# The long convolution as one transform of length 2048 with two DMA-shuffled stages, beside dilated sliding attention, on one core

## The chip, the cores and the metric

One core of one Trainium2 chip. The metric is device microseconds of one execution; the lower, the better.

## What is computed

Two independent parts, joined along the last axis. S = 2048 positions, D = 576 channels, bf16.

```python
# part A: 32 heads of 18 channels, 8 keys per query at distances 0, 2, .., 14
q, k, v = split(x @ wqkv)
logits = einsum("bhsd,bhswd->bhsw", q, k[s - 2*w]) * 18 ** -0.5   # masked where s - 2w < 0
a = einsum("bhsw,bhswd->bhsd", softmax(logits), v[s - 2*w]) @ wo
# part B: a 4-tap filter, a gate, a causal convolution over all 2048 positions, a gate
kv = (sum over t of k_pad[t:t+S] * shift_k[:, 3-t]) * v
y = irfft(rfft(pad(kv, 2*S)) * rfft(pad(ssm_k, 2*S)))[:S] + kv * ssm_D
b = q * y
out = concatenate([a, b], axis=-1)
```

## The kernel before

All work is cut into named jobs, and the string `ORDER` lists them in the order in which they are issued; each engine runs its own part of that list in program order. PSUM is used as four slots of two banks (`banks`); a job that needs a slot waits until the job that held it has been copied out.

Part A: `q`, `k`, `v` jobs project (columns of `wqkv` against the transposed x, 512 positions at a time; an `a` and a `b` half, the copy out at the end of `b`). `L` jobs are pair products of q and shifted k on VectorE, `G` jobs sum them over channels on TensorE. `sm..a` to `sm..d` are the softmax. `D` jobs spread the weights by DMA, `V` jobs weigh the shifted v on VectorE, `A` jobs sum over the eight keys on TensorE by an identity matrix, and `O` jobs multiply by `wo`, copy out and store. The first projections and the transposes of the first half of x stand ahead of ORDER.

Part B: `T` jobs (`taps`) form kv on VectorE in four blocks of 512 positions: multiply by the taps, add, gate. `M` folds each block with its mirror image. `x` jobs transform the four blocks, `F` and `K` fold and transform the filter's four blocks (loaded by `Lf` as DMA transposes), `U`, `Tx`, `Tk` and `ak`, `ax` prepare sums of parts, partly by DMAs that add. `p` jobs multiply a block's spectrum by a filter block's, with three products for one complex one; `z` jobs add the products up on TensorE, `i` and `b` transform back, `g` gates with q and stores. `Ex` loads ScalarE's table with Exp and Ln and `S1`, `I` make the transforms' tables from sines. ScalarE copies nearly all results out of PSUM. `Lk`, `Lv`, `Lf`, `Lw`, `Wl`, `Q` are loads, on SP's queue or POOL's.

Of the kernel before, what the change touches and what calls it, by code (L numbers as in the profile page):

```python
# [12 lines left out]
ALU = mybir.AluOpType  # L13
# [7 lines left out]
    T0 k03a' T1 S1 k03b I1 k02a k02b Lk2 Lv2 I0 k00a' Lk3 Lv3 M01 X5 k00b q10a Ex q10b Lf3 T2 Lo3 q13a' q13b  # L21
    k10a k10b T3 k13a' Lf2 k13b q12a q12b N2 Lo2 k01a M10 k01b Lf1 M00 k11a k11b q11a M11 q11b Lf0 N3 Lw SV L001
    k12a M20 k12b x001 M21 x021 q24a x020 q24b x000 Lo1 k24a Fr Lo0 Z2 N1 RG3 k24b RG2 F3 RG0 F2 L000 K310 G000
    K311 K210 K211 L002 K313 G001 RG4 F1 G002 L003 G003 K302 L004 G004 K301 L010 K212 L011 K303 K213 K203 N0 F0
    L012 K200 K300 G010 L013 K201 K312 K202 RG1 G011 G012 K113 K103 G013 L014 G014 K112 K102 K101 L100 K100 K010
    K111 K110 sm0a K001 K013 sm0b v24a' L101 v24b L102 G100 L103 G101 K012 sm0c sm0d U3 U2 K000 K011 K003 G102
    K002 D0 D1 v11a v11b G103 L104 G104 ak00 M30 v12a' v12b ak02 v01a ak01 L110 G110 M31 L111 G111 v01b v00a'
    L112 G112 L113 Wl v00b G113 x031 U1 L114 G114 V04 v10a' v10b A04 sm1a sm1b v02a v02b v03a' sm1c v03b x201
    V10 V11 sm1d V12 A10 v13a' v13b D2 x330 x310 x301 V13 A11 V20 V21 x200 x331 x230 x010 x221 A20 x321 V22 x210
    x011 V23 D3 V34 ax02 x220 x030 x300 D4 A21 V40 V41 A34 D5 O000' x211 V42 x320 x231 x111 x131 Tx2 A40 V43  # L30
    x120 x101 ax00 x130 ax01 V50 x121 x311 O001 A41 V51 O100' p000 x100 x110 O010 A50 V52 z000 O011' V53 O101
    A51 Tk2 p010 z010 ax10 O020' O021 p020 z020 O110' ak10 i000 p200 i02880 Q0 p100 z100 p101 p110 p111 Q1 z101
    i02881 i001 p121 p120 O111 z110 p201 z111 z120 p210 z121 O120 p211 z200 z210 z211 p212 z212 z201 p202 z202
    Tx3 p220 Tk3 p221 O030' p222 O121 b0288 z220 p301 z221 O031' p302 b00 z222 p303 i200 i100 g0 Q2 p300 y300
    p312 i12880 i201 i101 i12881 z300 z301 z303 p310 p311 y310 O130 b10 b1288 p313 g1 Q3 p322 O131' z310 p320
    z311 p321 z313 i22880 i300 b20 y320 p323 i22881 i301 b2288 g2 z320 z321 z323 b30 i3384L g30 g3384
"""

LHOMES = (0, 1, 2, 0, 1, 2, 0, 1, 2, 0, 1, 2, 0, 1, 0, 1, 0, 1, 0, 1)
VHOMES = (0, 1, 2, 0, 1, 2, 0, 1, 2, 0, 1, 2, 0, 1, 2, 0, 1, 2)  # L40
OHOMES = (0, 1, 1, 0, 2, 0, 1, 0)
JOINED = ("300 310 320").split()
PHOMES = (0, 1, 2, 3, 0, 1, 2, 3, 0, 4, 1, 2, 3, 0, 4, 1, 2, 3, 0, 1, 2, 3, 0, 1, 2, 3, 0, 1, 2, 3)


def view(t, offset, dims):

    return bass.AP(tensor=t.tensor, offset=t.offset + offset, ap=[list(t.ap[0])] + [list(d) for d in dims])


@with_exitstack
def kernel(
# [24 lines left out]

# [3 lines left out]

    NBL, BL = 4, 512  # L90


    GORD = [0, 2, 1, 3]
    HD = 288
    HB = 4 * D
    QTR = 768
    TH = 192
# [12 lines left out]
    jobs = {}  # L110

    xw = main.tile([128, 12 * HB], BF16, name="xw")
    XO = 8 * BL
    TB = main.tile([128, XO + 4 * BL], BF16, name="TB")
    TK = view(TB, 0, [[2 * BL, 2], [BL, 2], [1, BL]])
    TX = view(TB, XO, [[BL, 4], [1, BL]])
    TI = main.tile([128, 4, 2, 256], BF16, name="TI")
    XG = (9, 0, 3, 6)
    KVS = (0, 2, 1, 8)

    def kv_of(i):
        return view(xw, HB * KVS[i], [[D, 4], [1, D]])
# [26 lines left out]
    tB = sp1.tile([128, 8 * D], BF16, name="tB")  # L149
    skrow = tB[0:97, 0:4 * D]  # L150
# [17 lines left out]
    Ks = main.tile([128, 12 * HB], BF16, name="Ks")  # L168
    xnat = view(Ks, 4 * HB, [[HB, 4], [D, 4], [1, D]])
    n_all = view(Ks, 8 * HB, [[1, 4 * HB]]).bitcast(I32).rearrange("p (n f) -> p n f", n=9)  # L170

    def k_at(m, part):
        return 3 * HB * (3 - m) + HB * part

    def kTok(m):
        return view(Ks, k_at(m, 2), [[D, 4], [1, D]])
    kjs, vts = [], []

    def load_x(qtr):
        nc.sync.dma_start(xnat[:, qtr], xf[512 * qtr:512 * qtr + 512, :].rearrange("(sb p) c -> p sb c", p=128))  # L180
# [3 lines left out]
    def load_k(i):  # L184

        eng = nc.sync
        kj = sp1.tile([128, 7, D], BF16, name="kj", bufs=2)
        r0 = BL * i
        low = [(0, 64)]
        if i == 0:  # L190
            nc.gpsimd.memset(kj[0:1, 0:3, :], 0.0)
            nc.gpsimd.dma_start(kj[0:1, 3:7, :], kf[0:4, :].unsqueeze(0))
            low = [(1, 49), (49, 64)]
        for a, b in ((3, 7), (0, 3)) if i == 0 else ((0, 7),):
            for p0, p1 in low:
                eng.dma_start(kj[2 * p0:2 * p1:2, a:b], bass.AP(
                    tensor=kf.tensor, offset=kf.offset + (r0 + 4 * p0 - 3 + a) * D,
                    ap=[[4 * D, p1 - p0], [D, b - a], [1, D]]))
            eng.dma_start(kj[1:128:2, a:b], bass.AP(tensor=kf.tensor, offset=kf.offset + (r0 + 256 + 3 - a) * D,
                                                    ap=[[4 * D, 64], [-D, b - a], [1, D]]))  # L200
        kjs.append(kj)

    def load_v(i):
        vt = sp1.tile([128, 4, D], BF16, name="vt", bufs=2)
        nc.sync.dma_start(vt[0:128:2], vf[BL * i:BL * i + 256, :].rearrange("(p c) d -> p c d", c=4))
# [9 lines left out]
    fr_i = n_all[:, 8, :].rearrange("p (a b) -> p a b", a=4)
    rp_i = main.tile([128, 8], I32, name="rp_i")
    rp = main.tile([128, 8], FP32, name="rp")
    nc.gpsimd.iota(rp_i[:, 0:4], pattern=[[128, 4]], base=0, channel_multiplier=1)
    nc.gpsimd.iota(rp_i[:, 4:8], pattern=[[4, 4]], base=1, channel_multiplier=8)
    for gi, g in enumerate(GORD):  # L220
        sg = 1 - 2 * (g & 1)
        nc.gpsimd.iota(fr_i[:, gi, :], pattern=[[8 * sg, 128]], base=4096 * (g & 1) + sg * (2 * g + 1),
                       channel_multiplier=0)
    ones128 = sp1.tile([128, 128], BF16, name="ones128")
    nc.gpsimd.memset(ones128[:], 1.0)
    ident = main.tile([128, 128], BF16, name="ident")
    nc.gpsimd.affine_select(ident[:], ones128[:], pattern=[[1, 128]], compare_op=ALU.is_equal, fill=0.0,
                            base=0, channel_multiplier=-1)

    load_w(nc.sync, 0)  # L230
    load_x(1)

    def turn_x(h):

        r0 = 1024 + 512 * h
        nc.sync.dma_start(xnat[:, 2 + h, :, 512:576], xf[r0:r0 + 512, 512:576].rearrange("(sb p) c -> p sb c", p=128))
        nc.sync.dma_start_transpose(view(xw, 6 * HB + 512 * h, [[1024, 4], [1, 512]]), xf[r0:r0 + 512, 0:512])

    load_k(0)
# [896 lines left out]
```

## Time and profile before

| what | value |
|---|---|
| time, median of 3 runs | 206.23 us (206.15 to 206.59) |
| span of the profiled execution | 204.6 us |
| TensorE (PE) busy | 196.9 us, 96% |
| VectorE (DVE) busy | 192.3 us, 94% |
| ScalarE (ACT) busy | 155.6 us, 76% |
| GpSimd (POOL) busy | 60.8 us, 30% |
| DMA | 38.48 MB, mean 188 GB/s |

The span runs from the first to the last instruction of the profiled execution, and that execution's own time is known by this span only; the runs' times include what lies around it. "Busy" counts an engine's instructions of work. The chain that ended last is followed back from the last instruction, step by step, to what released each step. A group of instructions is shown as line, engine, operation, out<-in, shape and count, then busy time in us, mean ns of one, and the idle time before them.

### The profile page before, as it was taken

What the parts mean: (1) busy time and instruction counts of PE and PEld (TensorE: products, weight loads), DVE (VectorE), ACT (ScalarE), POOL (GpSimd) and SP (SyncE); (2) the same over time, 40 slices, a digit from 0 to 9 for tenths busy, and PEclk for the clock granted to TensorE, in tenths of its full rate; (3) what the DMA queues carried; (4) which work ended last, traced back from release to release, by engine and by line L of the source; (5) the groups of instructions that cost most, each with busy time, mean ns of one, the idle gap of its engine ahead of it and who ended that gap; (6) DMA issues with size and microseconds to landing.
All of it is one profiled execution on the core that took longest, in us unless ns stands there. A gap on an engine that the chain in (4) does not pass through costs nothing.

```text
span 204.6 us, 5004 instructions
## 1 busy us (share of the span) xinstructions
PE 196.9 (96%) x2074; PEld 109.9 (54%) x2074; DVE 192.3 (94%) x146; ACT 155.6 (76%) x223; POOL 60.8 (30%) x106
## 2 busy tenths in 40 slices
PE   7999999999989999999999999999999999999990
PEld 2543544334455646543245556776666767766660
DVE  7559999999999999999999999999999999899992
ACT  4788995678899999966578678886778767767760
POOL 8989500011348581400380000004090001030300
PEclk9999999999999999999999999999999999999997
DMA  6999899989509869999899990879989303944555
GB/s 197 280 293 306 175 289 373 214 177 281 169 3 146 111 82 185 167 180 222 157 235 216 248 244 34 141 183 334 186 227 233 100 28 122 227 130 145 153 182 150
DMA packets 34916, 38.48 MB, mean 188 GB/s; under 512 B 17523, under 2 KB 28911, under 8 KB 34894
## 3 DMA queue, kind: packets, MB, share of 16 engines
q1 hardware_dynamic: 26668, 24.29, 46.5%
q0 software_dynamic: 5760, 11.36, 29.5%
q10 hardware_dynamic: 2466, 2.51, 3.6%
q8 instruction: 16, 0.26, 0.5%
q14 instruction: 6, 0.05, 0.1%
HBM read 13.11 MB, written 4.72 MB: 87 GB/s over the span
## 4 chain that ended last, share of the span: by engine, by line
PE 88%; DMA 3%; ACT 2%; DVE 2%; issue 1%; SPq 1%; DVEq 0%
PE ps_proj L322 18%; PE ps_fx L682 8%; PE ps_wo L888 8%; PE ps_z L975 8%; PE ps_inv L1010 7%; PE ps_acc L824 7%; PE ps_fk L567 5%; PE ps_log L720 5%; DMA Ks<-in_A_x_dram 3%; PE ps_proj L333 3%; PE ps_proj L326 3%; PE ps_proj L439 3%; PE ps_fk L568 3%; PE ps_fold L545 2%; PE ps_wo L880 1%
## 5 line engine op out<-in xcount | busy, mean ns | idle before, releaser
L322 PE MATMUL ps_proj<-xw 128*128 128x512 bf16 x160 | 38.5, 380 | 0.0
L706 DVE TENSOR_TENSOR av<-qk 128x4096 bf16<-128x4096 bf16 (+1 forms) x16 | 31.7, 2014 | 0.1
L322 PEld LDWEIGHTS <-xw 128*128 128x128 bf16 x160 | 13.9, 98 | 19.4 <-issue 5.7
L988 ACT ACTIVATE av<-ps_z 128x768 bf16<-128x768 f32 x23 | 17.2, 811 | 6.5 <-PE ps_z L975 6.0
L517 DVE TENSOR_TENSOR tB<-kj,skb 128x4608 bf16<-128x4608 bf16 (+1 forms) x8 | 19.3, 2416 | 0.1
L950 DVE TENSOR_TENSOR qk<-xw,Ks 128x2304 bf16<-128x2304 bf16 x14 | 18.9, 1354 | 0.3 <-PE ps_z L975 0.3
L684 ACT ACTIVATE xw<-ps_fx 128x576 bf16<-128x576 f32 x32 | 18.6, 665 | 0.3 <-PE ps_fx L682 0.2
L618 ACT ACTIVATE Ks<-ps_fk 128x576 bf16<-128x576 f32 x32 | 18.6, 699 | 0.2 <-PE ps_fk L568 0.2
L355 ACT ACTIVATE qk<-ps_proj 128x1024 bf16<-128x1024 f32 x14 | 14.3, 1023 | 5.2 <-PE ps_proj L333 2.8
L888 PE MATMUL ps_wo<-qk 128*128 128x288 bf16 x128 | 17.9, 287 | 0.0
L626 POOL DMA_DIRECT2D Ks<-Ks x8 | 10.1, 1426 | 26.0 <-PE ps_back L1059 19.3
L682 PE MATMUL ps_fx<-xw,TB 128*128 128x288 bf16 x128 | 17.7, 287 | 0.0
L567 PE MATMUL ps_fk<-Ks,TB 128*128 128x384 bf16 x62 | 16.5, 327 | 0.1
L824 PE MATMUL ps_acc<-av,ident 64*64 64x512 bf16 x160 | 15.3, 378 | 0.0
L1010 PE MATMUL ps_inv<-av,TI 128*128 128x288 bf16 (+1 forms) x112 | 15.2, 292 | 0.0
L568 PE MATMUL ps_fk<-Ks,TB 128*128 128x192 bf16 x62 | 15.2, 246 | 0.0
L682 PEld LDWEIGHTS <-TB 128*128 128x128 bf16 x128 | 11.9, 98 | 5.9 <-issue 2.7
L888 PEld LDWEIGHTS <-qk 128*128 128x128 bf16 x128 | 11.7, 98 | 5.4 <-issue 2.7
L355 ACT ACTIVATE v<-ps_proj 128x1024 bf16<-128x1024 f32 x9 | 9.3, 1033 | 6.5 <-PE ps_proj L322 4.5
L813 DVE TENSOR_TENSOR av<-Ks,v 128x4096 bf16<-128x4096 bf16 x6 | 13.5, 2286 | 0.0
L827 ACT ACTIVATE qk<-ps_acc 128x1024 bf16<-128x1024 f32 x8 | 8.2, 1024 | 6.7 <-PE ps_acc L824 6.7
L1010 PEld LDWEIGHTS <-TI 128*128 128x128 bf16 x112 | 10.6, 98 | 4.2 <-issue 1.1
(195 smaller groups left out, 441.6 us busy)
## 6 DMA issues: line engine op xcount, KB each, us to landing
Ks<-Ks POOLq DMA_DIRECT2D x8, 576.0 KB, 7.8
TB<-av SPq DMA_DIRECT2D x12, 256.0 KB, 5.4
kj<-in_B_k_dram SPq DMA_DIRECT2D x6, 504.0 KB, 7.0
vt<-in_B_v_dram SPq DMA_DIRECT2D x8, 288.0 KB, 5.3
Ks<-av SPq DMA_DIRECT2D x8, 256.0 KB, 5.6
out_dram<-qk ACTq DMA_DIRECT2D x5, 288.0 KB, 3.7
Ks<-in_A_x_dram SPq DMA_DIRECT2D x2, 576.0 KB, 5.4
xw<-in_A_wqkv_dram SPq DMA_DIRECT2D x2, 576.0 KB, 6.2
```

The source lines that it names most:

```text
L322: nc.tensor.matmul(ps[:, jp, :], wq(kb, comp, 128 * ct, 128), xT(kb, 1024 * jj + 512 * jp, 512), **se)
L355: nc.scalar.activation(view(t, o + pad + 1024 * jj, [[512, 2], [1, 512]]), ps[:], ACT.Copy)
L517: tt(to, view(kj, row * D, [[D, n], [D, 4], [1, D]]), view(skb, row * D, [[D, n], [0, 4], [1, D]]), ALU.mult)
L567: nc.tensor.matmul(o[:, 0:2], w, rhs[:, 0:2], start=start, stop=stop)
L568: nc.tensor.matmul(o[:, 2], w, rhs[:, 2], start=start, stop=stop)
L618: nc.scalar.activation(view(Ks, k_at(m, cs ^ (m & 1)) + 96 * gi, [[768, 3], [384, 2], [1, 96]]), acc3(ps), ACT.Copy, scale=(PSG, MSG)[cs][ ...
L682: nc.tensor.matmul(ps[:, pm, 0:HD], TX[:, 2 * pm + c, 128 * gi:128 * gi + 128], kv[:, 2 * c + pm, HD * h:HD * h + HD], start=(c == 0), sto ...
L706: tt(view(P, at, [[step, 4], [256, nj], [1, 256]]), view(t, o + 256 * hh, [[0, 4], [512, nj], [1, 256]]), view(tk, ok + 2 + 8 * ug + 256 * ...
L824: nc.tensor.matmul(acc[64 * o:64 * o + 64, h, :], ident[64 * h:64 * h + 64, 64 * h:64 * h + 64], view(P[s], 256 * u, [[2048, 2], [1, 256]] ...
L888: nc.tensor.matmul(ps[:, r, 0:HD], oT(hh, j + 2 * r, t)[:, o:o + 128], wo[:, t // 2, t % 2, HD * h:HD * h + HD], start=(t == 0 and not fli ...
L950: tt(product_home(n), view(xw, HB * XG[i] + QTR * t, [[HB, 3], [1, QTR]]), view(Ks, k_at(j - i, 0) + QTR * t, [[HB, 3], [1, QTR]]), ALU.mult)
L1010: nc.tensor.matmul(ps[:, c, 0:n], TI[:, sl, pm, 128 * c:128 * c + 128], Yall(j % 2, pm, sl, slice(c0, c0 + n)), start=(pm == 0 and sl == 0 ...
```

## The change

Part B is written anew, and ORDER with it; the jobs of part A keep their content.

- `t` (8) and `s` (12) take the place of `T`: VectorE multiplies by the taps, TensorE adds the four taps by an identity matrix into PSUM, VectorE gates out of PSUM. Half of the rows hold positions in reversed order, so k and v are loaded in blocks of 32 partitions.
- `x` (18) and `f` (18) are a first stage of the transform, 64 rows at a time; after each, DMAs on POOL's queue put 144 KB each into four partitions (32 DMAs for x, 32 for f). `X` and `Y` (18 each) are the second stage, in place, with a small matrix. `F` (8) turns the filter, now loaded straight, by TensorE transposes.
- `p` (18) multiplies four parts on VectorE, `z` (18) is the inverse's first stage with 32 more such DMAs, `y` (9) its last stage, gated by q out of PSUM and stored.
- Tables: two index tables are multiplied out on POOL, and `Sw`, `Sx`, `Sf` take sines of them on ScalarE; `Tw`, `Tt` transpose.
- The v projection reads its weights 9 columns apart, so the regrouping copies (`RG`) go. `Ex` stands in the last line of ORDER.

The order of issue begins, turns and ends so:

```
Sw t01 t00 Lw s00 s01 s02 k03a k00a k00b t10 k02a k02b k03b XT Sx t11 s10 s12 s11 q10a t20 q10b Sf k01a k01b
Tw q11a q11b t21 s22 s20 s21 x0 k12a k12b x1 x2 q12a q12b x3 q13a q13b t30 t31 s30 s31 L002 x4 x5 k10a k10b
...
G111 F2 Dr f0 G112 D0 G113 G114 F1 f1 f2 sm1a f3 F4 sm1b F5 F6 F3 f4 F7 f5 f6 f7 D1 f8 V04 sm1c sm1d f9 f10
X3 f11 f12 V10 V11 A04 V12 D2 X1 f13 f14 f15 f16 f17 X11 A10 V13 D4 X13 X9 V20 A11 Y0 V21 Y2 V22 Y14 p0 Y1
...
O000 p16 p17 z16 z17 O010 V43 A41 z8 V50 Tt Q11 O001 V51 V52 A50 V53 O011 y3 y0 y5 A51 y1 O020 O021 O030
O031 y2 y4 y6 O110 O111 O100 Ex O101 y7 O130 O131 y8 O120 O121
```

New functions, cut to their core:

```python
def tap_sums(c, p):
    ...
    kv = view(R5, 2 * D * c + lo, [[8 * D, 2], [1, 384]])
    tt(kv, ps[:, :, 0:384], kv, ALU.mult)

def first_stage(name, T, src, ring, size, place, to, at):
    ...
    for a, w in cut(at, 512, size):
        copy_out(name, view(WR, ring + a % size, [[size, 2], [1, w]]), ps[:, :, a - at:a - at + w])
    ...
                nc.gpsimd.dma_start(to[pi:128:32, :].rearrange("p (r c) -> p r c", c=D),
                                    view(WR, ring + size * hh + D * g % size, [[1, D]]))

def second_stage(name, w, t, p):
    ...
            nc.tensor.matmul(ps[64 * o:64 * o + 64, h, :], w[r], view(t, HALF * o + 512 * p, [[1, 512]])[r],
                             start=True, stop=True, tile_position=(64 * h, 64 * o))
    copy_out(name, view(t, 512 * p, [[HALF, 2], [1, 512]]), ps[:])

def spectral_product(p):
    tt(view(*product_home(p), [[1024, 2], [512, 2], [1, 512]]), view(VB, 512 * p, [[HALF, 2], [0, 2], [1, 512]]),
       view(FB, 512 * p, [[0, 2], [HALF, 2], [1, 512]]), ALU.mult)

def last_stage(u):
    ...
    qB = view(FB, 1024 * u, [[512, 2], [1, 512]])
    tt(qB, ps[:], qB, ALU.mult)

def indices(at, m):
    nc.gpsimd.tensor_tensor(view(words(at, 2048), 0, [[32, 64], [1, 32]]), view(m, 0, [[1, 64], [0, 32]]),
                            view(vec, 0, [[0, 64], [1, 32]]), ALU.mult)

-    load_v(0)
+    load_v(0, 4)      # 8 DMAs of 32 partitions, in place of 2
     load_k(1)         # 4 DMAs, in place of 2
     turn_x(0)
     turn_x(1)
-    load_v(1)
+    load_k(2)
+    load_k(3)
+    load_v(4, 4)
```

`copy_out` is ScalarE's copy here for every job, as the list of exceptions is empty.

More of the change, by code (lines that the diff above doesn't have):

```diff
@@ L31 @@
[L31 to L35, printed above, removed]
@@ L110, with job @@
     jobs = {}
[L112 to L122, printed above, removed]
+    late = set(VEVAC.split())
+    def job(name, fn, *args):
+        assert name not in jobs
+        jobs[name] = partial(fn, *args)
@@ new lines, in copy_out @@
+    def copy_out(name, to, of):
+        if name in late:
+            nc.vector.tensor_copy(to, of)
+        else:
+            nc.scalar.activation(to, of, ACT.Copy)
+    qk = main.tile([128, 4 * S + 1024 + 4 * KW + KWH], BF16, name="qk")
+    VB = main.tile([128, 2 * HALF], BF16, name="VB")
+    FB = main.tile([128, 2 * HALF], BF16, name="FB")
+    WR = main.tile([128, 2 * HALF + 8 * D], BF16, name="WR")
+    R5 = main.tile([128, HALF], BF16, name="R5")
+    VV = main.tile([128, 4 * KW + KWH], BF16, name="VV")
@@ L215 @@
[L215 to L223, printed above, removed]
@@ new lines, in pieces_of, with load_v, load_filter @@
+    def pieces_of(t, pitch, c0, hh, s, b, i0, n):
+        f = 2 * i0 + (hh if b == 0 else 1 - hh)
+        return rows_of(t, pitch, c0, 63 - 16 * b - f if s else 16 * b + f, n, -2 if s else 2)
+    def load_v(i0, n):
+        for p, hh, s in BLOCKS:
+            for b in range(2):
+                nc.sync.dma_start(view(R5, 8 * D * b + D * i0, [[D, n], [1, D]])[p:p + 32],
+                                  pieces_of(vf, D, 0, hh, s, b, i0, n))
+    def load_filter(kb):
+        at = (R5, 2048 * kb) if kb < 4 else (WR, HALF)
+        p = min(128, 576 - 128 * kb)
+        nc.sync.dma_start(view(*at, [[1, S]])[0:p], B_ssm_k[128 * kb:128 * kb + p, :])
@@ new lines, in turn_walls, with turn_table @@
+    def turn_walls():
+        ps, slot = banks("ps_w", BF16)
+        for n in range(2):
+            nc.tensor.transpose(ps[:, n, 0:128], view(pre, 128 * n, [[1, 128]]), ident[:])
+        for n, t in enumerate((W2X, W2F)):
+            nc.scalar.activation(t[:], ps[:, n, 0:64], ACT.Copy)
+        slots.append(slot)
+    def turn_table():
+        ps, slot = banks("ps_t", BF16)
+        for g in range(16):
+            nc.tensor.transpose(ps[:, g // 8, 128 * (g % 8):128 * (g % 8) + 128], view(T1X, 128 * g, [[1, 128]]), ident[:])
+        nc.scalar.activation(view(T1X, 0, [[1024, 2], [1, 1024]]), ps[:], ACT.Copy, scale=1.0 / 2048.0)
+        slots.append(slot)
@@ L483 @@
     project_first(0, 2)
-    sines[2]()
-    for n in range(2):
-        project_first(1, 2 * n)
-        sines[3 - 3 * n]()
-    def job(name, fn, *args):
-        assert name not in jobs
-        jobs[name] = partial(fn, *args)
+    project_first(1, 0)
+    project_first(1, 2)
     project(0, 1)
@@ L538, in mirror @@
-    def mirror(i, n):
-        kv = kv_of(i)
-        pss, held = zip(*[banks("ps_fold") for _ in range(2)])
-        for pm in range(2):
-            for h in range(2):
-                for e in range(2):
-                    nc.tensor.matmul(pss[pm][64 * e:64 * e + 64, h, 0:HD], fold[:, 64 * pm:64 * pm + 64],
-                                     kv[:, 2 * n + e, HD * h:HD * h + HD], start=True, stop=True, tile_position=(0, 64 * e))
-        for pm in range(2):
-            nc.scalar.activation(halves(kv[:, 2 * n + pm, :]), pss[pm][:, :, 0:HD], ACT.Copy)
-        slots.extend(held)
@@ L612, in filter_unit @@
-    def filter_unit(m, cs, gi):
-        ps, slot = banks("ps_fk")
-        lower = cs == 0 and gi in (1, 2)
-        for c in range(2):
-            mm3(ps, TK[:, c, cs, 128 * gi:128 * gi + 128],
-                thirds(other(m) if lower and c == 0 else kTok(m)[:, 2 * (1 - cs) + c, :]), c == 0, c == 1)
-        nc.scalar.activation(view(Ks, k_at(m, cs ^ (m & 1)) + 96 * gi, [[768, 3], [384, 2], [1, 96]]), acc3(ps),
-                             ACT.Copy, scale=(PSG, MSG)[cs][m] * 2.0 ** 1.5 / 1024.0)
-        slots.append(slot)
@@ L658, in exponential @@
+    for u in range(9):
+        job(f"y{u}", last_stage, u)
+    for b in range(2):
+        for n in range(2):
+            job(f"Q{b}{n}", load_q, b, 4 * n, 4)
     def exponential():
@@ L893, in output @@
         st = view(*homes_st[OHOMES[4 * j + sb]], [[D, 2], [1, D]])
-        nc.scalar.activation(st[:, :, HD * h:HD * h + HD], ps[:, :, 0:HD], ACT.Copy)
+        copy_out(f"O{j}{sb}{h}", st[:, :, HD * h:HD * h + HD], ps[:, :, 0:HD])
         slots.append(slot)
@@ L1100 @@
-    job("ak10", third_sum, Ks, k_at(1, 0), HB)
-    job("ax10", third_sum, xw, HB * XG[1], HB)
     for name in ORDER.split():
         jobs.pop(name.rstrip("'"))(*([True] if name[-1] == "'" else []))
-    assert not jobs and len(slots) == 4
+    assert not jobs and len(slots) == 4, (list(jobs), slots)
 _INS = ['A_x', 'A_wqkv', 'A_wo', 'B_q', 'B_k', 'B_v', 'B_shift_k', 'B_ssm_k', 'B_ssm_D']
```

773 lines of the change are left out of this document (286 added, 487 removed).

## The prediction

> **What bounds the kernel now.** I read first the share of the chain that ended last, then busy time by stage, then the chain's pieces for what each kind of matrix product costs.
>
> ```profile
> PE 88%; DMA 3%; ACT 2%; DVE 2%; issue 1%; SPq 1%; DVEq 0%
> ...
> 0.00:18.40 18.40, 16.78 (x96) 7.32 (x96) 12.80 (x23) 12.85 (x16) 16.48 (x48) 1.00 0.94 277
> 18.40:63.80 45.40, 44.65 (x324) 20.19 (x324) 44.67 (x29) 37.96 (x52) 13.01 (x25) 1.00 0.88 206
> 63.80:113.00 49.20, 49.20 (x466) 24.45 (x462) 48.84 (x36) 40.95 (x59) 18.68 (x21) 1.00 0.93 172
> 113.00:155.00 42.00, 42.00 (x533) 27.62 (x530) 41.97 (x25) 32.47 (x50) 7.54 (x9) 1.00 0.83 202
> 155.00:204.60 49.60, 44.23 (x667) 30.34 (x665) 43.98 (x37) 31.36 (x48) 5.13 (x7) 0.98 0.53 143
> sum 204.60, PE 196.85 PEld 109.91 DVE 192.25 ACT 155.58 POOL 60.84; mean PE 39.37 PEld 21.98 DVE 38.45 ACT 31.12 POOL 12.17
> ```
>
> TensorE (PE) is 88% of the chain. From 18.4 to 155 us it is busy for 135.85 of 136.6 us, and VectorE (DVE) for 135.48. The two are level; ScalarE (ACT) has 20 to 23% left. A change pays only if it relieves both, and it must not fill ACT in a stretch where PE and DVE wait for it.
>
> ```profile
> 18.59 1.83 PE ps_proj L322 x8
> 20.42 0.57 PE ps_ti L397 x16
> 22.82 0.32 PE ps_proj L333 x2
> 33.20 3.56 PE ps_proj L322 x16
> 53.77 1.85 PE ps_proj L326 x16
> 64.93 0.98 PE ps_log L720 x16
> 111.27 1.85 PE ps_acc L824 x32
> 145.08 0.65 PE ps_z L975 x16
> 160.30 0.98 PE ps_wo L888 x8
> 185.33 0.49 PE ps_back L1059 x16
> ```
>
> Columns: start, time, piece. The work whose place ORDER sets starts at about 18.4 us. A 512-column product costs 0.23 us on the whole array, two at once on half arrays the same (L326), four on quarters (L824: 32 in 1.85). The least pitch of any instruction is 0.031 us (L1059), with 128 columns 0.036 (L397).
>
> **What goes and what comes.** On DVE, rows by form:
>
> ```profile
> L950 DVE TENSOR_TENSOR qk<-xw,Ks 128x2304 bf16<-128x2304 bf16 x14 | 18.9, 1354 | 0.3 <-PE ps_z L975 0.3
> L517 DVE TENSOR_TENSOR tB<-kj,skb 128x4608 bf16<-128x4608 bf16 (+1 forms) x8 | 19.3, 2416 | 0.1
> L706 DVE TENSOR_TENSOR av<-qk 128x4096 bf16<-128x4096 bf16 (+1 forms) x16 | 31.7, 2014 | 0.1
> L813 DVE TENSOR_TENSOR av<-Ks,v 128x4096 bf16<-128x4096 bf16 x6 | 13.5, 2286 | 0.0
> L748 DVE TENSOR_TENSOR av<-av 128x2048 bf16<-128x2048 bf16 x1 | 1.2, 1225 | 0.0
> L1020 DVE TENSOR_TENSOR TB<-ps_back,TB 128x768 bf16<-128x768 f32 x1 | 1.0, 954 | 0.0
> L468 DVE COPY xw<-ps_x 128x512 bf16<-128x512 bf16 x2 | 0.7, 406 | 0.0
> ```
>
> Gone are 30 spectral products of 1.354 (40.6 us), the joins and third sums, and the tap adds. Left as they are: pair products and weighings (20 and 18 of about 2.28, the four short pair products about half: 41.3 and 41.2) and softmax with small things (8, by forms like L748's). New: 8 tap products of 2.5 (20.0), 12 tap sums out of PSUM of about 0.92 by L1020 (11.0), 8 filter copies of 1152 elements (0.75, an estimate from L468's 0.406 for 512, between that row itself and 0.91, its multiple: 6.0), 18 products of 2048 elements of 1.22 (22.0), 9 last gates of 1024 from PSUM of 1.2 (10.8). Sum 160 us; back to back they overlap by about 3%, so 155: some 37 less than the 192.25 of now.
>
> On PE the folds, block transforms, sums and inverses go. After 18.4 us there are by the chain's rows: 23 projection units of 1.83 + 0.3 (49.2), pair sums 20 of 0.5 (10.7), weighted sums (8 of 1.85, two of 1.0: 16.8), outputs 16 of 0.98 + 0.13 (18), tap sums 12 of 0.69 (16 quarter products of 384, as L975: 8.3), 36 first stages of 0.26 (9.4), 36 second stages of 0.25 (9.0), 18 inverses of 0.47 (8.5), 9 last stages of 0.52 (4.7), and 320 small transposes for the filter: 0.033 each, between the two pitches (10.6; 9.9 to 11.5). With 3.5 of small things, 149 us, against 180 busy now by the four later stages.
>
> On ACT the rows of time show the price of a copy:
>
> ```profile
> 21.23 1.01 ACT L355 ACTIVATE qk<-ps_proj 128x1024 bf16<-128x1024 f32 x1
> 22.13 1.08 ACT L401 ACTIVATE TI<-ps_ti 128x512 bf16<-128x512 f32 x2
> ...
> 28.27 1.28 ACT L659 ACT_TABLE_LOAD   x1
> 29.56 0.20 ACT L660 ACTIVATE warm<-pib 128x1 f32<-128x1 f32 x1
> ```
>
> 1024 elements take 1.01, but the next starts 0.90 later: 0.92 each in a row. Five groups of 18 such copies (both first stages, both second stages, inverse) are 83 us, in place of the block transforms' copies; in all ACT keeps about 155 with its start. So no engine has less than before on ACT, and 26 to 37 us leave the others. Total work is not what will bound; its order is.
>
> **Where the time goes: one chain through the queues.** Engines run in program order and PSUM has four slots, so PE cannot run far ahead of ACT. I split ORDER where the sums change hands.
>
> *To f5 on PE.* All projections, tap sums, the pair sums, the filter's transposes, x stages, 11 X and 6 f stages stand ahead: 49.2 + 8.3 + 10.7 + 6.2 + 2.7 + 10.6 + 1.8 = 89.5 us, while ACT has 67 there and DVE 85. This stretch is PE-bound, DVE close behind: I add 1.5, the 2% that PE idles in such a stretch now (0.75 of 45.4).
>
> *Loads on SP.* One issue costs about 0.63.
>
> ```profile
> 11.28 0.59 SPq L205 DMA_DIRECT2D vt<-in_B_v_dram  x1
> 15.36 6.30 SPq L237 DMA_TRANSPOSE xw<-in_A_x_dram  x1
> ...
> 21.70 0.57 SPq L236 DMA_DIRECT2D Ks<-in_A_x_dram  x1
> 22.32 1.97 SPq L237 DMA_TRANSPOSE xw<-in_A_x_dram  x1
> ...
> kj<-in_B_k_dram SPq DMA_DIRECT2D x6, 504.0 KB, 7.0
> vt<-in_B_v_dram SPq DMA_DIRECT2D x8, 288.0 KB, 5.3
> out_dram<-qk ACTq DMA_DIRECT2D x5, 288.0 KB, 3.7
> ```
>
> load_v(0) becomes 8 issues in place of 2 and load_k(1) 4 in place of 2, ahead of turn_x: eight more issues, 5.1 us, so its first transpose moves from 15.4 to 20.5 and its second tail from 21.7 to 26.8. XT needs that tail: reached on PE at 28 (18.4 + 9), it waits to 30.5 or 32, and behind it in PE's and ACT's queues stand Sx, the second tap sums and q10a. The k of chunk 2 is issued by 32 and lands 7 later at 39; t20 and t21 end at 43 to 44. PE would come to their sums s22 at 36, after XT's wait at 39: 7 us lost in all, and nothing covers them (0 if the loads come as early as now; 12 if k takes 2 more and v 3: its second half, issued by 39.5, lands at 45, and three PSUM slots are held until then). Behind these on SP stand Lw and the filter's five loads, which are wanted only after 60 us: covered.
>
> *From f5 to z8 on ACT.* Copies of 1024: 13 f, 7 X, 18 Y, 18 z (56 of 0.92: 51.5), 8 of weighted sums 6.7, a softmax part 0.8, two outputs 1.1: 60 us, while PE has 34 and DVE 55. Here ACT decides. Ex, the job that loads the table with Exp and Ln together, moves from the 19th place to the last line of ORDER. In the runs of now there is one load after the sines (L659). Later, Exp and Ln of each softmax may each bring their own: two of 1.28 us (2.6) fall into this stretch, two more into the first where ACT has time, and Ex's own into the tail. Between 0 and 4 loads in the stretch; I take the two.
>
> [...] The load here is 1.28, and the next activation starts 1.29 after it: no drain is seen. [...]
>
> *From z8's copy to the end.* Its two shuffles go out on POOL; y3 needs all of WR. The nearest row is a plain 144 KB copy on the same queue:
>
> ```profile
> L650 POOL DMA_DIRECT2D Ks<-Ks x3 | 1.7, 570 | 24.5 <-DVE xw L520 20.0 <-DMA Ks<-in_B_ssm_k_dram 4.5
> ...
> DMA to landing us min/median/max: 2.9/3.2/4.7
> ```
>
> Two issues of 0.54 and 3.2 to land: y3 starts 5 to 6 us after the copy, meanwhile PE has Tt, O001, A50 and O011 (5.2) and DVE four weighings (9.2), so the wait is covered. Then PE holds A51, 9 y and 12 outputs: 1.85 + 4.7 + 13.4 = 20. The last copy 0.55, issue 0.4, landing 3.7: 31 from z8 to the end.
>
> Sum: 18.4 + 89.5 + 1.5 + 7 + 60 + 2.6 + 31 = 210.0 us of span. The span now is 204.6 and the median of the runs 206.23; with the same 1.6 around it, 211.6.
>
> The other steps. 96 shuffles of 0.54 to 0.63 are 52 to 60 us of POOL, spread over three phases of 20 to 36 us with 19 each: covered, by a narrow margin in f. They write four partitions each, which no row shows: landing between 2.9 (a 128-partition copy) and 7.0 (k's loads); I take 3.2, as size and queue are the same; at 7.0 the barriers at X0, Y0 and y3 cost 4 each, less 2 of cover. Bytes: the z phase moves 4.7 MB of shuffles plus about 6 of q, wo, spreads and output in 36 us, 300 GB/s, where the first stage now has 277 at a share of 0.94: no room. The accumulating DMAs and DMA transposes of the filter go, which costs nothing and frees that time. The strided weights of v (9 apart) in place of regroup: 0 to 0.1 us more per load, 72 loads; hidden behind products of 0.23, so 0. Copies from L355 regrouping (6.6 of ACT) go, in a stretch where ACT has slack: 0.
>
> **Rivals.** *Faster, 203 us or less.* The loads come as early as now and the tables cost ACT nothing: 210.0 - 7 - 2.6 = 200.4, 202 with the 1.6. For it: both are waits that I place by counting issues, and the queue accepted 0.6 apart. It decides if the PE idles under 3 us before s32.
>
> *Index tables late.* Two products of 128x2048 int32 move to POOL; Sx and Sf on ACT wait for them, and with ACT everything that needs a PSUM slot.
>
> ```profile
> 5.58 0.45 POOL L250 TENSOR_SCALAR_AFFINE_SELECT flip<-ones 128x128 bf16<-128x128 bf16 x1
> 12.39 1.40 POOL L286 TENSOR_SCALAR_AFFINE_SELECT flip<-ones 128x128 bf16<-128x128 bf16 x1
> ...
> 12.28 1.36 DVE L517 TENSOR_TENSOR xw<-kj,skb 128x2304 bf16<-128x2304 bf16 x1 [4.16 <-DMA kj<-in_B_k_dram]
> ```
>
> The same instruction takes 0.45 before DVE's products begin at 12.28 and 1.40 under them. At 0.45 for 128 elements they cost 7 us each alone, at 1.40 22 each under DVE. I reckon POOL free for them at 14 and DVE's tap products at it a third of the time: done at 24 and 35, just as Sx (28, or 31 after XT's wait) and Sf (32, or 35) come. If all falls under DVE, they are done at 58: Sf waits 23, the tap sums behind it cover 5, and the time is 229. [...]
>
> *Shuffles slow.* At 7.0 or more to land and with DMA full, X0, Y0 and y3 wait 3 to 6 each, the last behind z's whole queue: 211.6 + 10, 222. Against it stands L650's 3.2; for it, that four partitions take what 128 take there.
>
> **Chances.** Forecast, 207 to 217: 0.38. Faster rival, 196 to 205.8: 0.32. Within 0.2% (about what a measurement of this kernel can tell from no change): 0.05. Tables late, 217 to 231: 0.12. Shuffles slow, 215 to 228: 0.13. So faster 0.32, same 0.05, slower 0.63. Range 198 to 225, which leaves a tenth on each side; the forecast's own is 207 to 217.
>
> **What would show it.** DVE near 155 to 162 busy and PE near 165; PE dense to about 117 us with gaps only before 60, at XT and s22; ACT without gaps from 117 to 180, with loads of tables at the softmax; a tail of 30 us that PE fills. Wrong would be: ACT idle for more than 10 us between f5 and z8 (then shuffles or DVE set the pace), PE waiting for Sx or Sf, a first stretch that ends before 110, or filter transposes at over 0.05 us each (6 us more).

## The result, and the profile after

The kernel with the change takes 367.41 us (median of 4 runs, 367.31 to 368.35) against 206.41 beside it: 1.780 times as long (1.776 to 1.784). It was forecast slower, but at 211.6 with 225 as the upper end. Some executions of one kernel run in a slower state; the times below are those of the others, which for E2 and E6 leaves one run each, and E2's rows are from a slower run.

From the page after, the line of busy time, and a table by stage cut at the forecast's own marks: start of the ordered work, f5 on PE, z8 on PE, end. Columns of the table: window, length, busy time of PE, PEld, DVE, ACT and POOL with instruction counts, granted clock, DMA share, GB/s.

```profile
PE 207.6 (57%) x2140; PEld 102.3 (28%) x2140; DVE 166.2 (45%) x112; ACT 163.2 (45%) x181; POOL 99.3 (27%) x184
...
0.00:18.40 18.40, 17.13 (x92) 8.10 (x92) 5.57 (x9) 10.96 (x14) 16.50 (x59) 1.00 0.95 230
18.40:145.40 127.00, 101.76 (x1160) 50.70 (x1158) 86.46 (x57) 73.52 (x78) 31.77 (x46) 0.88 0.58 112
145.40:323.40 178.00, 59.15 (x582) 26.22 (x579) 56.83 (x36) 62.90 (x69) 47.44 (x74) 0.61 0.55 92
323.40:366.60 43.20, 29.51 (x320) 17.32 (x312) 17.31 (x12) 15.80 (x21) 3.59 (x6) 0.87 0.60 140
```

The sums of work came out near: DVE 166 for 160, ACT 163 for 155. PE has 207.6 for 165, part of it at a granted clock of 0.61 in the stretch where it mostly waits. ACT has 62.90 busy between f5 and z8, where 60 was forecast, but the stretch is 178.0 us long and not 62.6. So little work was missed; waits were. They stand in the list of waits (engine, line, waited for: total us, times, longest) and in the DMA part (last number: median us from issue to landing):

```profile
DVE WR L610 <- DMA WR<-VB: 77.7, 8, 14.1
ACT VB L111 <- PE ps_i L621: 54.7, 6, 15.4
...
POOL VB L563 <- ACT WR L111: 31.7, 11, 7.9
...
POOL FB L563 <- DMA FB<-WR: 23.3, 9, 3.7
...
ACT WR L111 <- DMA VB<-WR: 17.0, 9, 4.2
...
q0 software_dynamic: 14912, 17.41, 28.3%
...
VB<-WR POOLq DMA_DIRECT2D x32, 144.0 KB, 8.2
FB<-WR POOLq DMA_DIRECT2D x32, 144.0 KB, 12.9
WR<-VB POOLq DMA_DIRECT2D x32, 144.0 KB, 8.1
```

The 96 shuffles, the DMAs into four partitions, land after 8.1 to 12.9 us (medians), not 3.2. And a new wait appears that the prediction does not have: DVE's spectral product (L610, into WR) waits eight times, 77.7 us in all, for an inverse's shuffle (WR<-VB). DVE's own timeline shows the rhythm: a product or two, then nothing until shuffles have landed.

```profile
230.63 1.23 DVE L610 TENSOR_TENSOR WR<-VB,FB 128x2048 bf16<-128x2048 bf16 x1 [12.79 <-DMA WR<-VB]
247.08 1.23 DVE L610 TENSOR_TENSOR WR<-VB,FB 128x2048 bf16<-128x2048 bf16 x1 [14.09 <-DMA WR<-VB]
261.12 1.23 DVE L610 TENSOR_TENSOR WR<-VB,FB 128x2048 bf16<-128x2048 bf16 x1 [11.67 <-DMA WR<-VB]
```

Against the forecast's marks the excess is 29.0 us up to f5 (145.4 for 116.4), 115.4 from f5 to z8 (178.0 for 62.6) and 12.2 in the tail (43.2 for 31), 156.6 together.

### The profile page after: what moved, and what is told of

Read it like the earlier page. It is cut to its first block, busy times and chain, and to the rows that moved or that the text cites. A ratio compares the mean times of both kernels' runs of the same rounds, so it can differ in the third digit from the quotient of the medians.

```text
span 366.6 us, 5213 instructions
## 1 busy us (share of the span) xinstructions
PE 207.6 (57%) x2140; PEld 102.3 (28%) x2140; DVE 166.2 (45%) x112; ACT 163.2 (45%) x181; POOL 99.3 (27%) x184
## 2 busy tenths in 40 slices
DMA packets 34568, 40.86 MB, mean 111 GB/s; under 512 B 18096, under 2 KB 28400, under 8 KB 34544
## 3 DMA queue, kind: packets, MB, share of 16 engines
q0 software_dynamic: 14912, 17.41, 28.3%
## 5 line engine op out<-in xcount | busy, mean ns | idle before, releaser
L610 DVE TENSOR_TENSOR WR<-VB,FB 128x2048 bf16<-128x2048 bf16 x12 | 14.6, 1224 | 91.1 <-DMA WR<-VB 77.7
L111 ACT ACTIVATE WR<-ps_f 128x1024 bf16<-128x1024 f32 (+1 forms) x38 | 36.3, 982 | 37.8 <-DMA VB<-WR 17.0
L686 DVE TENSOR_TENSOR FB<-qk 128x4096 bf16<-128x4096 bf16 (+1 forms) x20 | 40.8, 2074 | 21.9 <-PE ps_log L700 13.2
L628 POOL DMA_DIRECT2D WR<-VB x32 | 21.4, 675 | 65.7 <-issue 28.5
L779 DVE TENSOR_TENSOR qk<-R,VV 128x4096 bf16<-128x4096 bf16 x11 | 24.8, 2287 | 24.2 <-DMA R<-AT 15.1
L563 POOL DMA_DIRECT2D FB<-WR x32 | 21.3, 671 | 40.1 <-DMA FB<-WR 23.3
L563 POOL DMA_DIRECT2D VB<-WR x32 | 22.1, 697 | 32.9 <-ACT WR L111 31.7
L312 PE MATMUL ps_proj<-WR 128*64 128x512 bf16 x176 | 26.9, 448 | 0.3 <-ACT qk L111 0.3
L111 ACT ACTIVATE qk<-ps_acc 128x1024 bf16<-128x1024 f32 (+1 forms) x10 | 9.4, 940 | 36.8 <-PE ps_acc L790 24.8
L519 DVE TENSOR_TENSOR VV<-FB,AT 128x4608 bf16<-128x4608 bf16 x6 | 21.9, 3675 | 8.3 <-POOL VB L381 8.3
L790 PE MATMUL ps_acc<-qk,ident 64*64 64x512 bf16 x176 | 21.2, 565 | 5.5 <-ACT WR L111 4.8
L309 PE MATMUL ps_proj<-WR 128*128 128x512 bf16 x96 | 23.9, 394 | 0.0
L656 DVE TENSOR_TENSOR FB<-ps_y,FB 128x1024 bf16<-128x1024 f32 x9 | 10.6, 1220 | 17.5 <-PE ps_y L651 10.7
## 6 DMA issues: line engine op xcount, KB each, us to landing
FB<-WR POOLq DMA_DIRECT2D x32, 144.0 KB, 12.9
R<-AT SPq DMA_DIRECT2D x16, 256.0 KB, 13.9
```

What stands on the lines that cost most here:

```text
L111: nc.scalar.activation(to, of, ACT.Copy)
L309: nc.tensor.matmul(ps[:, jp, :], wq(kb, comp, 128 * ct, 128), xT(kb, 1024 * jj + 512 * jp, 512), **se)
L312: nc.tensor.matmul(ps[64 * e:64 * e + 64, jp, :], columns(kb, ct, e), xT(kb, 1024 * (jj if ct < 4 else e) + 512 * jp, 512), tile_position= ...
L519: tt(view(*tap_home(c, m), [[4 * D, 2], [D, 4], [1, D]]), view(FB, D * (4 * c + 2 * m), [[D, 2], [D, 4], [1, D]]), view(skb, 2 * D * m, [[ ...
L563: nc.gpsimd.dma_start(to[pi:128:32, :].rearrange("p (r c) -> p r c", c=D), view(WR, ring + size * hh + D * g % size, [[1, D]]))
L610: tt(view(*product_home(p), [[1024, 2], [512, 2], [1, 512]]), view(VB, 512 * p, [[HALF, 2], [0, 2], [1, 512]]), view(FB, 512 * p, [[0, 2], ...
```

## The experiments

The theories on the lost time. *A, same tile:* products and shuffles share the tile WR, in different columns, and the product is held until the shuffles are down. *B, the shuffles themselves are slow.* *C, the low granted clock is a cause of its own.* *P*, the first tap product is held by POOL's index tables. Under B: *T*, it is the destination in few partitions; *Q*, it is the queue or the packet.

**E1, the products' ring in a tile of its own.** The ring of 8 x 576 columns at the end of WR becomes a tile RG. The ring of the filter's first stage lay across that border, so its copies out of PSUM are split in two as well (ACT then has 199 instructions for 181, and 164.0 us busy for 163.2). The edit, cut to its core:

```diff
-    WR = main.tile([128, 2 * HALF + 8 * D], BF16, name="WR")
+    WR = main.tile([128, 2 * HALF], BF16, name="WR")
+    RG = main.tile([128, 8 * D], BF16, name="RG")
...
-        return (WR, RING + 2048 * n) if n < 2 else (T1F, 0)
+        return (RG, 2048 * n) if n < 2 else (T1F, 0)
```

> The ring behind WR's first 18432 columns becomes a tile of its own; order, sizes and addresses' use stay. Theory A (the products in the ring are held back by the inverse's shuffles, which write other columns of the same tile): the 77.7 us that VectorE waits on WR<-VB go, the stretch from the first product to y3 shrinks from some 130 us to 60 to 75, and the time falls from 367 to 295 to 310. Theory B (the shuffles' own slowness sets the pace, landing 8 us each): the wait only moves to y3 and the time stays above 350. Theory C (the low granted clock of 0.5 to 0.6 there is a cause of its own): clock and time stay.

316.78 us (314.61 to 318.95), ratio 1.532 (1.507 to 1.557). The wait of products on shuffles is gone, the last product starts at 241.7 in place of 316.7, and 50.6 us are saved; the time stays above A's 295 to 310. The mean granted clock rose from 0.752 to 0.804 although nothing was done to it, against C. The rest of the 77.7 comes back after it; waits and stages of E1:

```profile
DVE FB L662 <- DMA FB<-in_B_q_dram: 26.1, 1, 26.1
PE ps_y L657 <- DMA FB<-in_B_q_dram: 26.1, 1, 26.1
...
201.00:250.00 49.00, 33.67 (x399) 15.35 (x395) 36.95 (x26) 38.50 (x44) 20.61 (x34) 0.76 0.82 128
250.00:283.00 33.00, 6.94 (x88) 4.33 (x88) 6.85 (x4) 5.39 (x6) 13.21 (x21) 0.63 0.99 132
...
q0 software_dynamic: 14912, 17.41, 38.4%
...
VB<-RG POOLq DMA_DIRECT2D x32, 144.0 KB, 8.6
WR<-VB POOLq DMA_DIRECT2D x32, 144.0 KB, 10.7
```

From 250 to 283 the DMA share is 0.99 at only 132 GB/s. The 26.1 us before the last stage are put down to q's loads, which stand among the last shuffles on POOL; but the product L657 reads WR and T1X and no q, so it is the shuffles into WR that PE waits for, and E8, with q's loads on another queue, shows the same wait under the shuffles' name. That the products' wait is a false one is shown, and it is the smaller part; what is left is B.

**E2, E1 with every second shuffle on SP's queue.** The first stages' edit; the inverse's is the same, with `h`:

```diff
-                    nc.gpsimd.dma_start(to[pi:128:32, :]...
+                    (nc.sync if hh else nc.gpsimd).dma_start(to[pi:128:32, :]...
```

> As the run with the ring in a tile of its own, and every second shuffle is issued on SP's queue in place of POOL's. Theory A2 (after the false waits, the first stages are paced by at most eight shuffles in flight on POOL's queue): the waits of POOL and ACT on FB<-WR and VB<-WR (23 and 33 us) fall below 15 in sum and the time is 20 to 35 below that run. Theory B2 (the 16 DMA engines are full with packets into four partitions): landing times grow and the time stays within 8 of it. SP could also be blocked by a spread ahead: then up to 15 slower.

348.38 us, 31.6 slower than E1, more than any case of the expectation. SP carries the spreads and loads too; a shuffle behind them waits for what they wait for, here a spread (L766) for VectorE:

```profile
PE ps_y L657 <- DMA WR<-VB: 45.1, 1, 45.1
...
SPq L766 <- DVE qk L785: 19.8, 2, 17.7
```

So taking issues off POOL is no remedy; E2 tells no more than that.

**E3, the kernel after with four adjacent destination partitions** (4p to 4p + 3) in place of p, p + 32, p + 64, p + 96; which rows meet in a partition changes.

> The changed kernel, but each shuffle writes four adjacent partitions in place of four that are 32 apart (rows are then permuted wrongly in the transform's middle). Theory A (the ordering comes from the stride over partitions): products no longer wait on the shuffles, as with the tile split, 295 to 310. [...] If landing stays near 8, the stride is not what makes it slow.

452.84 us, ratio 2.190 (2.164 to 2.216). The ring lies in WR as in the change, and yet no product waits for a shuffle: sharing the tile is not enough for the false wait; in these runs it came only where the destinations skip partitions too (77.7 us in the change, none here). It is still 85 us slower than the change:

```profile
POOL FB L563 <- DMA FB<-WR: 64.0, 17, 8.2
...
q0 software_dynamic: 14912, 17.41, 56.7%
...
VB<-WR POOLq DMA_DIRECT2D x32, 144.0 KB, 15.9
FB<-WR POOLq DMA_DIRECT2D x32, 144.0 KB, 27.9
WR<-VB POOLq DMA_DIRECT2D x32, 144.0 KB, 18.3
```

Same bytes, same packets, same queue: the place of the destination alone doubles the landings and takes 56.7% of 448.9 us (255 us of all 16 engines) in place of 104. That turned the question to the destination.

**E4, the kernel after with the two index products about 8 us earlier on POOL.**

> The changed kernel with the two index products on POOL some 8 us earlier, ahead of VectorE's first tap product. Theory P (the first tap product, 9.3 us in place of 2.55, is held by POOL's two products from 14.9 to 22.1): it takes 2.6, s00 starts 6 to 7 us earlier, and the first x stage 3 to 7 earlier; the end moves by 0 to 7. Rival: it waits for k's load; then it stays at 9.

365.37 us (363.30 to 367.44), no change clear of the spread. DVE's tap products in the kernel after (ns min/median/max, first and last start in us), with POOL's index products (start, time), and then in E4:

```profile
L519 DVE TENSOR_TENSOR VV<-FB,AT x6: 2544/2551/9304, 15.2 to 52.7; 128x4608 bf16<-128x4608 bf16 x6
...
14.88 7.22 POOL L371 TENSOR_TENSOR VB<-VB 128x2048 int32<-128x2048 int32 x2
```

```profile
L520 DVE TENSOR_TENSOR VV<-FB,AT x6: 2546/2552/2583, 15.1 to 50.5; 128x4608 bf16<-128x4608 bf16 x6
```

In the kernel after, POOL's two products run from 14.88 to 22.10, and the tap product that DVE starts at 15.2 ends at 24.5: 9,304 ns for 2,551. With the tables earlier it takes 2,583 at most, the tap sums start 6.7 us earlier on PE (20.3 for 27.0) and x0 6.5 earlier (42.3 for 48.8); by X0 (107.5 for 108.4), which waits for shuffles, all but a microsecond is gone again. P is shown, as a cost that does not reach the end here.

**E5, E7, E6, E14: other destinations for each shuffle, on top of E1.** The edit is the destination's pattern; E5, whose copy stays in its own 128 partitions, leaves the exchange of rows out, the others change which rows meet in a partition. In the expectations of E9, E10 and E12 below two letters are new: D is the distance and N the number of partitions.

```diff
-   to[pi:128:32, :].rearrange("p (r c) -> p r c", c=D)                                      # E1: 4, 32 apart
+   view(to, D * pi, [[1, D]])                                                               # E5: all 128
+   to[pi % 8:128:8, ...][:, 8 * (pi // 8):8 * (pi // 8) + 8]                                # E7: 16, 8 apart
+   to[32 * (pi // 8) + pi % 8:32 * (pi // 8) + 32:8, ...]                                   # E6: 4, 8 apart
+   to[16 * (pi % 8):16 * (pi % 8) + 16, ...][:, 8 * (pi // 8):8 * (pi // 8) + 8]            # E14: 16, adjacent
```

> E1's kernel (the ring in a tile of its own) with each of the 96 shuffles turned into a copy of the same 144 KB from the same 128 partitions to the same 128 partitions, on the same queue, in the same place, 128 packets of 1152 B; what it leaves out is the exchange of rows between partitions. In E1 a packet of POOL's queue took 38.4% x 16 x 312.8 / 14912 = 129 ns. Theory T (a write into four partitions is what is slow): a packet falls to 55 to 75 ns (before's SP queue: 46.5% x 16 x 204.6 / 26668 = 57 ns for 911 B), landings from 8.6, 10.7 and 13.5 us to 3 to 5, the last product's y3 comes less than 35 us after the last inverse's output, and the time is 225 to 260 us. Theory Q (POOL's queue, or the packet's size, is what is slow; before's POOL queue took 29.5% x 16 x 204.6 / 5760 = 168 ns for 1972 B, which is 98 ns for 1152 B): a packet stays at 95 to 130 ns and the time at 290 to 317 us.

> E1's kernel with each shuffle written to 16 partitions 8 apart, 8 packets of 1152 B to each, in place of 4 partitions with 32 packets to each; which rows meet in a partition is changed by it. Theory T (the number of destination partitions that a transfer writes at one time is what limits it): a packet between the straight copies' and E1's 129 ns, 60 to 90 ns, and the time 230 to 280 us. Theory Q (queue or packet size): as E1, 115 to 135 ns and 300 to 320 us.

> E1's kernel with each shuffle's four destination partitions 8 apart inside one block of 32 (32b + r, + 8, + 16, + 24) in place of 32 apart; which rows meet in a partition is changed by it, the sizes and the order are not. Four adjacent partitions gave 273 ns for a packet of POOL's queue, four partitions 32 apart 129 ns. If the limit belongs to a block of 32 partitions, this is as slow as the adjacent ones: 240 to 290 ns, 410 to 455 us. If it belongs to a smaller group of partitions (8 or fewer), this is as E1: 115 to 145 ns, 305 to 330 us.

> [...] Which rows meet in a partition is changed. [...]

E5 takes 230.36 us, ratio 1.116 (1.109 to 1.122): theory T's range, with the queue, the bytes and the places in the order unchanged.

```profile
q0 software_dynamic: 5696, 17.26, 26.0%
...
VB<-RG POOLq DMA_DIRECT2D x32, 144.0 KB, 2.3
WR<-VB POOLq DMA_DIRECT2D x32, 144.0 KB, 4.0
FB<-WR POOLq DMA_DIRECT2D x16, 144.0 KB, 6.5
FB<-RG POOLq DMA_DIRECT2D x16, 144.0 KB, 7.2
```

The nanoseconds for a mean packet in those expectations were a bad yardstick. E5 has 9,216 packets fewer than E1, all under 512 B (8,880 such packets for 18,096) and together 0.15 MB (17.26 for 17.41), so a shuffle to four partitions carries 96 packets of, by an estimate from these numbers, 16 B beside its data; the mean mixes the two. Landings and times are compared instead. E7 (245.70) went as T expected, E6 (291.80) fits neither a block of 32 (410 to 455) nor "as E1" (305 to 330), and E14 (290.67), with as many partitions as E7, would be like E7 if their number alone counted: it is like E6.

E5 changes one thing more: a straight copy writes 576 columns of every partition, so a later stage need not wait for all 32 shuffles of its phase, and the last stage starts at 198.7, when the last shuffle has only just been issued (198.5). How much of the 86.4 us from E1 to E5 that is was not run. E7 and E14 have no such difference: same columns, same queue, 5,696 packets each as in E5, 16 partitions each, and only which 16 they are costs 45.0 us. That leaves theory Q, queue or packet, no part in those 45.0 us.

**E9 and E13, the transfers by themselves.** Zeros as output and nothing else, then 144 KB copies, each after the one before has landed, later bursts of eight. In E9 the instructions of two kinds were interleaved, so that most copies were not alone; E13 runs them in the order written.

> The disputed cost by itself: a kernel that writes zeros as its output (all of the computation is left out) and then sends 144 KB copies of 128 source rows on POOL's queue, four of each kind, each after the one before has landed: to 4 partitions that are 1, 2, 4, 8, 16 and 32 apart, to 16 partitions 8 apart, and to all 128; then bursts of eight. E3, E1 and E6 gave 273, 129 and 90 ns for a packet with destinations 1, 32 and 8 apart, which no distance orders. [...] Theory D (what counts is the distance or the block of 32): 2 apart is near 1 apart, 16 apart is as good as 8 apart, and the bursts are equal. Theory N (the number of destination partitions alone): all six kinds with four partitions are equal within 20%. [...]

> E9 again (zeros as output, all of the computation left out) with the copies in the order written, so that four of each kind are really alone, and with a kind more: 16 adjacent partitions. [...]

E13, one line of the kernel for each kind; from the top 4 partitions 1, 2, 8, 16 and 32 apart, 16 adjacent, 16 partitions 8 apart, and all 128:

```profile
L71 POOL DMA_DIRECT2D TA<-Z x4 | 3.0, 738 | 1.3 <-POOL TA L67 0.9
DMA to landing us min/median/max: 7.3/7.4/8.0
L74 POOL DMA_DIRECT2D TA<-Z x4 | 2.8, 689 | 1.2 <-POOL TA L67 1.2
DMA to landing us min/median/max: 4.6/5.4/5.6
L80 POOL DMA_DIRECT2D TA<-Z x4 | 2.8, 690 | 1.2 <-POOL TA L67 1.2
DMA to landing us min/median/max: 3.9/4.4/4.5
L83 POOL DMA_DIRECT2D TA<-Z x4 | 2.8, 689 | 1.2 <-POOL TA L67 1.2
DMA to landing us min/median/max: 4.6/4.9/5.7
L86 POOL DMA_DIRECT2D TA<-Z x4 | 2.7, 686 | 1.2 <-POOL TA L67 1.2
DMA to landing us min/median/max: 4.7/5.5/5.7
L89 POOL DMA_DIRECT2D TA<-Z x4 | 2.2, 539 | 1.2 <-POOL TA L67 1.2
DMA to landing us min/median/max: 3.0/3.0/3.0
L92 POOL DMA_DIRECT2D TA<-Z x4: 527/530/534, 187.6 to 196.1; - x4
DMA to landing us min/median/max: 2.3/2.3/2.3
L95 POOL DMA_DIRECT2D TA<-Z x4 | 2.2, 550 | 1.2 <-POOL TA L67 1.2
DMA to landing us min/median/max: 2.0/2.0/2.0
```

The order is not that of distance: 2, 16 and 32 apart are alike (5.4, 4.9, 5.5), 8 apart is faster (4.4; 4 apart the same), adjacent slowest (7.4). Nor is it that of the number of partitions alone: four take from 4.4 to 7.4, 16 take 2.3 when they are 8 apart and 3.0 when they are adjacent. So it matters which partitions a transfer writes; what the slow sets have in common is not shown by these runs. What separates four partitions 8 apart (4.4) from 16 adjacent ones (3.0) can be their number, their places or the 96 small packets; no run separates these. In E9 a copy to four partitions, alone, kept the DMA share at 0.14 to 0.16, one to 16 partitions 8 apart at 0.23 and one to all 128 at 0.19.

Side by side (bursts of eight from E13: first issue to the last landing):

| destination | alone | burst of 8 | kernel | time |
|---|---|---|---|---|
| all 128 | 2.0 us | 6.2 | E5 | 230.4 |
| 16, 8 apart | 2.3 | not run | E7 | 245.7 |
| 16, adjacent | 3.0 | 11.5 | E14 | 290.7 |
| 4, 8 apart | 4.4 | 12.1 | E6 | 291.8 |
| 4, 32 apart | 5.5 | 13.4 | E1 | 316.8 |
| 4, adjacent | 7.4 | 19.9 | E3 (ring in WR) | 452.8 |

In the whole kernel the order of the times is that of the copies alone, but the steps are not: E6 and E14 are 1.1 us apart, with 4 partitions and with 16, as their bursts are near each other too (12.1 and 11.5), while E7 with 16 other partitions takes 45 us less than E14.

**E10 and E12, an order that spreads successive shuffles over the partitions.** In E13 eight shuffles to four partitions 32 apart took 24.8 us when their first partitions were 0 to 3, twice over, and 13.4 when they were 0, 4, 8 and on to 28; with 8 apart it was 14.9 for 0 to 3 twice over, and 12.1 for 0 and 4 in each block of 32. E10 is E1, and E12 is E6 with E4's tables and the exponential earlier, both with the inverse's shuffles placed so that those of successive rows g begin three or more partitions apart and not next to each other, after the faster bursts; which rows meet in a partition is changed.

```diff
+    def place_z(g, h):                                  # E10, on E1
+        return 4 * ((g + 4 * h) % 8) + g // 8 + 2 * h
-   WR[g + 16 * h:128:32, ...]
+   WR[place_z(g, h):128:32, ...]
```

> [...] Theories D and N, or if what the queue has before it decides: WR<-VB stays at 10 to 11.5 and the time at 314 to 320.

> [...] Which rows meet in a partition is changed. [...] Theory N: 288 to 295. [...]

Neither gained by it. E10: 316.25 us (314.28 to 318.47), in the range of D and N, WR<-VB at 11.1 (E1 10.7). E12: 294.74 us, in N's range, though WR<-VB fell a little (8.4, E6 8.9); its x0 is 6.3 us earlier than E6's (43.0 for 49.3), its last x 2.1 later (93.6 for 91.5). So the spread that shortens a burst by itself does not explain the pace in the kernel. What paces successive shuffles inside the kernel, where spreads, loads and shuffles share the engines, stays open.

**E8, the change with its repairs:** E1, E4's tables, the exponential earlier, q's loads on SP.

> The change with every repair that the runs point to: the ring in a tile of its own (E1), the index tables about 8 us earlier (E4), ssm's exponential moved behind the first f's sine so that one table load fewer stands between products, and the loads of q on SP's queue in place of POOL's, so that POOL's list holds the shuffles alone. If the 96 shuffles' packets (12288 x 129 ns over 16 engines = 99 us, and the spreads and loads beside them) set the time, it stays near E1: 295 to 320 us. If waits between engines still do, 250 to 285 us.

309.44 us, ratio 1.499 (1.492 to 1.506). With four destination partitions 32 apart the last stage still waits for shuffles, and q's loads are no longer in the way:

```profile
PE ps_y L658 <- DMA WR<-VB: 24.6, 1, 24.6
```

**E11, E5 with E4's tables and the exponential earlier.** The exchange of rows is left out, as in E5.

> E5 (each shuffle a copy to the same 128 partitions; the exchange of rows is left out) with E4's early index tables and ssm's exponential behind the first f's sine: what is left of the forecast's 211.6 when shuffles land as a plain copy does. In E4 the tables gave 6.5 us at the start, which the shuffles took back. If the rest of the forecast's chain is right, the 6.5 now reach the end with a table load: 221 to 225 us against E5's 230.4, and x0 at 42 in place of 48.5. If another wait (the spreads in the DMA queues, at a share of 0.80 to 0.90 in the last stages) takes it back, 227 to 231.

225.51 us, ratio 1.091 (1.087 to 1.094); x0 at 42.7. By stage, cut again at f5 and z8:

```profile
18.40:117.80 99.40, 92.13 (x1157) 48.46 (x1157) 79.30 (x56) 71.17 (x82) 29.96 (x72) 0.98 0.56 148
117.80:188.60 70.80, 46.59 (x578) 22.64 (x578) 56.35 (x35) 59.74 (x80) 38.72 (x72) 0.86 0.91 218
188.60:223.90 35.30, 28.12 (x320) 16.67 (x312) 17.16 (x12) 14.43 (x19) 4.36 (x8) 0.95 0.64 180
```

Once a shuffle costs what a plain copy does, the forecast's chain is nearly there: f5 at 117.8 (forecast 116.4), ACT 59.74 busy from f5 to z8 (60), that stretch 70.8 (62.6), tail 35.3 (31). E11 has no table load between f5 and z8, where the forecast counts 2.6, so like for like that stretch is 10.8 over. No version reaches 206.4, and E11, without the exchange of rows, does not compute the convolution.

## Why the prediction was wrong

The sign was right, but for a reason that the forecast did not have: it was slower by 5 us for waits on loads and for table loads, and the 161 us measured are nearly all others. The size was wrong by 156 us. Largest first, each as measured in the order of the runs named (another order was not run):

- **Shuffles priced as a plain copy: 86.4 us (E1 to E5).** The step that failed is "landing between 2.9 ... and 7.0 ...; I take 3.2, as size and queue are the same". Size and queue were the same, the destination was not. I had written that no row shows a write into four partitions, and then took the row that was nearest in the things that did not matter. The upper end was no bound either: 8.1 to 12.9 were measured, 13.4 for eight in E13 against 6.2. Part of the 86.4 can be the waits that E5 loosens.
- **Their effect counted at three barriers, not as a pace.** The rival "Shuffles slow" named the mechanism, with a chance of 0.13, but charged 3 to 6 us at X0, Y0 and y3. In the profile after, ACT's copies wait for the ring that a shuffle still reads (17.0), POOL's next shuffle for a landed one (23.3): waits all along a phase and not only at its end. The sentence "300 GB/s ... no room" was the right alarm, and no time was drawn from it: E1 moves 132 GB/s at a share of 0.99.
- **A wait not seen: 50.6 us (E1).** The products' ring lies in the tile that the inverse's shuffles write, with destinations 32 partitions apart. The columns differ, the order was enforced all the same; with adjacent destinations (E3) it was not. The prediction followed data, not tiles, and costed ACT's queue behind z alone.
- **Index tables: 4.9 us, with the exponential's move (E5 to E11).** The rival had them late and ACT waiting at Sx and Sf. They were not late: 3.6 us each where the rival had 7, done at 22.1. The two rows of the mask (0.45 and 1.40) were read as "DVE slows POOL", and here POOL held DVE, through both of its products: the tap product begun at 15.2 took 9,304 ns and ended at 24.5, 2.4 after the second index product (22.1), and in E4, with them earlier, 2,583 at most. The prediction looked at one direction only. How the 4.9 us divide between the tables and the exponential was not run.
- **What is left, 13.9 us (E11 over the forecast):** 1.4 to f5, 8.2 from f5 to z8, 4.3 in the tail. From f5 to z8 ACT idles 11 us, put down for the most part to products of PE (`ps_f` 3.8, `ps_acc` 3.5); what holds those up was not followed.

Right were the sums of work on DVE and ACT (PE's was low: 184.0 even in E11, for 165), the two table loads of 1.28 for a softmax part, and the filter's transposes. ACT's slack before the change was misread: the rows give 16 to 23%, not 20 to 23. The sign named as proof of a wrong forecast, ACT idle for more than 10 us between f5 and z8, is what came: 115 us of it. The 7 us for SP's loads came in another place. In E11 PE reaches XT at 30.9 without a wait; it idles 1.9 us at 20.3 for the first tap products, and 1.9 at 25.3 and 2.5 at 45.7 for PSUM slots of tap sums whose gate on VectorE waits for a load. That 6.3 us came for 7, and with them the 116.4 within 1.4, is partly luck.

## What to carry to other kernels

When a transfer changes shape, price it by the partitions it writes, not by bytes and queue alone: 144 KB into four partitions took 4.4 to 7.4 us alone where 128 partitions took 2.0, and 96 of them set the pace of this kernel. A step that "no row shows" and that occurs 96 times deserves its worst price times its count as a rival, not one latency at each barrier. And look which tile an instruction writes, not only which data it needs: a ring kept in the spare columns of a tile into which DMAs write at every 32nd partition cost 50 us.

## What the runs showed of the hardware

- The time of a 144 KB copy into four partitions did not follow the distance between them: 2, 16 and 32 apart (5.4, 4.9, 5.5 us in E13) were slower than 4 or 8 apart (4.4), and adjacent ones slowest (7.4).
- A DMA share near 1 did not mean many bytes: 0.99 at 132 GB/s in E1 from 250 to 283 us, where its first 18.4 us have 0.94 at 227.
- Two POOL products in a row, each with two inputs in SBUF, held a DVE product with two inputs in SBUF until both were done: 9,304 ns for 2,551 in the kernel after, and 2,583 at most in E4, where they run earlier.
- PE's granted clock fell to 0.61 where it waited most (E11 in the same stretch: 0.86); over the kernel PE was 207.6 us busy in place of E11's 184.0.
